# Attention kernel: constant rows on two engines, output weights split once, maxima and sums transposed in one round

## The chip, the cores and the metric

The kernel runs on one core of a Trainium2 chip. The core has five engines with a queue of instructions each: TensorE (PE in the profile; its weight loads are PEld), VectorE (DVE), ScalarE (ACT), GpSimd (POOL) and SyncE (SP), which only issues transfers. Each engine works through its queue in order, and semaphores tie the queues together. The metric is the device time of one execution in microseconds, as the median of several runs.

## The reference

Two kinds of layer alternate, four in all, on an input of 2048 rows of 576 numbers. The change lies in the attention layers.

```python
x = x + _A_ref(_layernorm(x), wqkv, wo)      # attention
x = x + _B_ref(_layernorm(x), w_r, w_i)      # a filter between two Fourier transforms
x = x + _A_ref(_layernorm(x), wqkv, wo)
x = x + _B_ref(_layernorm(x), w_r, w_i)

def _A_ref(x, wqkv, wo):                      # H = 32 heads of Dh = 18, window W = 256
    q, k, v = (x @ wqkv) in 32 heads
    scores = einsum("bhqd,bhkd->bhqk", q, k) * Dh ** -0.5
    scores = where((0 <= i - j) & (i - j < 256), scores, -1e9)
    o = einsum("bhqk,bhkd->bhqd", softmax(scores), v)
    return o @ wo
```

## The kernel before

Every attention layer (`layer_a`) runs three stages, and `layer_b` follows as the fourth.

*The opening* normalizes and transposes the 16 blocks of 128 rows (`xh` and `xl`, the high and low parts of the transposed rows) and computes the values, with one software pipeline over the blocks; `f2` is its last stage.

*The attention loop.* The 32 heads form eight stacks n of four heads (two halves hp of the partitions, two pairs). A stack's queries and keys lie in `qs` and `ks`, at partitions 64 hp and above: 54 rows of split queries or keys, and above them constant rows that memsets have set, 0.0 in `qs` and 1.0 in `ks`. Row 63 of each half of `qs` takes minus the maximum of each query's scores, so that with the row of ones in `ks` one matmul gives the score less its maximum. There are two buffers each of `qs` and `ks`; the memsets are done once per layer, between eight first projections (`proj`, 14 matmul steps each), 64 memsets over the two layers.

The loop runs over time steps t; step t = 16n + i handles block i of stack n. In each step PE does

- four matmuls E (L834) for key block i of stack n against three query blocks i to i+2. ACT takes their exponentials (L835), and POOL cuts off what lies outside the window (L837, L840);
- four matmuls S (L802) for step t+10, whose maxima DVE takes (L804);
- the matmuls U (L854) of exponentials with values for step t-2;
- a few matmul steps `pj` (L741) of later projections, as a table `goal` spreads them. A projection ends in steps 5, 10, 14, 19, 24, 28, 33, 37, 42, 47, 51, 56, 60, 65, 70, 74, 79, 83, 88, 93, 97 and 102. Its result is split on ACT, DVE and POOL, and SP writes it to memory (`qk_d<-sg`, L756).

At every step that is a multiple of 4 SP is also given the twelve `stack_load` transfers (L781) for a chunk of the next stack, `qs<-qk_d` and `ks<-qk_d`; at steps 4 mod 16 the values `vq` as well (L786).

A chunk c is four blocks. Two jobs come once per chunk. `m_rows` transposes the chunk's maxima on PE (`tpm`, L810), ACT negates them into `mt` (L812), and SP writes them into row 63 in four small transfers, `qs<-mt` (L817). They are needed by the E of step 16n + 4c - 2 (16n for the first chunk). `norm` transposes the finished U with its sums (`tpo`, L864), DVE divides (L867, L869), and SP stores the result (`o_d<-o`, L874). Both jobs wait in a list `due`: `m_rows` comes in at steps 2 mod 4, `norm` at steps 3 mod 4. Each step takes at most one job from the list, and none where a projection ends in that step.

*The output stage* (class `Out`) multiplies by the output weights, split into a high and a low part. The split is made in the loop's last steps of each layer: `room` (step 104) loads the raw weights (L474), and at steps 108, 110, 112, 114 and 116 `split` makes one fifth on ACT (L478) and POOL (L479).

The order of all queues is the order of the program text (a manual schedule); nothing is reordered later.

Of the kernel before, what the change touches and what calls it, by code (L numbers as in the profile page):

```python
# [8 lines left out]
F32 = mybir.dt.float32  # L9
F32R = mybir.dt.float32r  # L10
# [5 lines left out]
S, D = 2048, 576  # L16
# [432 lines left out]
class Out:  # L449
# [6 lines left out]
    def room(self):  # L456
        self.rh = rh = self.bp.tile([128, 5 * S], F32R, tag="xh", name="oroom")
        self.rl = f = self.bp.tile([128, 4 * S], F32, tag="xl", name="ofree")
        self.w = {"h": rh[:, 0:2880], "l": rh[:, 2880:5760]}
        self.oT = [rh[:, 5760 + 896 * k:6656 + 896 * k] for k in range(3)]  # L460
        self.oL = [rh[:, 8448 + 256 * k:8704 + 256 * k] for k in range(3)]
        self.gc = rh[:, 9216:9472].rearrange("p (a c) -> p a c", a=2)
        small = f[:, 8130:8170]
        self.st = [small[:, 12 * k:12 * k + 12] for k in range(2)]
        self.mv = [small[:, 24 + 2 * k:26 + 2 * k] for k in range(4)]
        self.rs = [small[:, 32 + k:33 + k] for k in range(4)]
        self.nb = [small[:, 36 + k:37 + k] for k in range(4)]
        self.raw = f[:, 0:2880]
        self.x = [f[:, 576 * k:576 * k + 576] for k in range(5)]
        self.o = [f[:, 2880 + 448 * k:3328 + 448 * k] for k in range(3)]  # L470
        self.tl = [f[:, 4224 + 128 * k:4352 + 128 * k] for k in range(4)]
        self.o7 = f[:, 4736:6784].rearrange("p (n e) -> p n e", n=NT)
        for a, b in ((0, 2), (2, 5)):
            self.nc.sync.dma_start(self.raw[:, a * D:b * D], self.wo_d[:, a * D:b * D])  # L474

    def split(self, k):
        c = slice(k * D, k * D + D)
        self.nc.scalar.copy(self.w["h"][:, c], self.raw[:, c])  # L478
        self.nc.gpsimd.tensor_sub(self.w["l"][:, c], self.raw[:, c], self.w["h"][:, c].bitcast(F32))  # L479

    def consts(self):

# [95 lines left out]
            self.turn(u, tp[:, 0], self.nc.scalar, tp[:, 1, 0:128])  # L578


def layer_a(tc, src, dst, wqk_d, wv_d, wo_d, dc_d, gc_d, dram, copy, wvs, second, spectral):
    nc = tc.nc
    V, A, T, P = nc.vector, nc.scalar, nc.tensor, nc.gpsimd
    SC = float(DH) ** -0.5
# [6 lines left out]
    with ExitStack() as ctx:  # L591
# [30 lines left out]
        with tc.tile_pool(name="a1", bufs=2) as wp, tc.tile_pool(name="a1p", bufs=2, space=PSUM) as pp:  # L622
            if not second:
                wraw = wp.tile([128, 5, D], F32, name="wvraw", bufs=1)
            wh = wp.tile([128, 5, D], F32R, name="wvh", bufs=1)
            wl = wp.tile([128, 5, D], F32R, name="wvl", bufs=1)
            st = wp.tile([128, NT, 2, 6], F32, name="st", bufs=1)
# [50 lines left out]
            def f1(t, h):  # L678
# [5 lines left out]
                if t == 6 and not second:  # L684
                    for j, w in enumerate((wh, wl)):
                        nc.sync.dma_start(wvs[j].bitcast(F32), w.rearrange("p a b -> p (a b)").bitcast(F32))

            def f2(t, h):
                if t in (10, 12):
                    w_split((t - 10) // 2)  # L690
                c = slice(t * 128, (t + 1) * 128)
                ps = pp.tile([128, 2, 512], F32, tag="v", name=f"vps{t}", bufs=2)
                ks = k_steps()
                for i, (wk, p, xk) in enumerate(ks):
                    w = wh if p == "h" else wl
                    for n in range(2):
                        T.matmul(ps[:, n, 0:288], xT(xk, c), w[:, wk, n * 288:(n + 1) * 288],
                                 start=i == 0, stop=i == len(ks) - 1)
                vt = vts[t % 3]
                for n in range(2):  # L700
                    A.copy(vt[:, 16 * n:16 * n + 16, 0:18], ps[:, n, 0:288].rearrange("p (h d) -> p h d", d=18))
                nc.sync.dma_start(v_d[:, :, t].rearrange("n p e -> p n e"), vt.rearrange("p (n h) e -> p n (h e)", n=NQ))
# [4 lines left out]
        with ExitStack() as c2:  # L707
# [8 lines left out]
            qs, ks_ = [], []  # L716
# [159 lines left out]
            for k, (i, c) in enumerate(((0, 0), (1, 0), (0, 1), (1, 1), (0, 2), (0, 3), (1, 2), (1, 3))):  # L876
                for f in proj(i, c, "E" if k % 2 else "pj"):
                    f()

                for b in (32, 96):  # L880
                    P.memset(ks_[i][b:b + 32, :, 512 * c:512 * c + 512].bitcast(F32), 1.0)
                    P.memset(qs[i][b:b + 32, :, 512 * c:512 * c + 512].bitcast(F32), 0.0)
                if k in (2, 4):
                    stack_load(0, k // 2 - 1)
            NX = NQ * NT
# [8 lines left out]
                    goal[t] = 84 + 14 * m - (-14 * (t + 1 - a) // (b - a))  # L894

            OB = NX - 8
            out = Out(nc, ident, eps, bp, ov, o7v, srcv, dstv, wo_d, dc_d, gc_d)

            for t in range(-LEAD, NX + 2):

                if t + LEAD in (0, 2):
                    stack_load(0, 2 + (t + LEAD) // 2)
                n, c = divmod(t + 20, NT)
                if c % 4 == 0 and 0 < n < NQ:
                    stack_load(n, c // 4)
                if t + LEAD == 5:
                    v_load(0)
                if t + 12 in range(NT, NX, NT):
                    v_load((t + 12) // NT)

                want = goal.get(t, len(pj))
                ends = done // 14 != want // 14
                more, done = pj[done:want], want
                for pair in range(2):
                    for hp in range(2):
                        if 0 <= t < NX:
                            exps(t, pair, hp)
                    for hp in range(2):
                        if t + LEAD < NX:
                            score_max(t + LEAD, pair, hp)  # L920
                    while later:
                        later.pop()()
                    if pair == 0 and 0 <= t - 2 < NX:
                        pv(t - 2)
                    if pair == 0 and t < 2:
                        for f in more[:(len(more) + 1) // 2]:
                            f()
                        more = more[(len(more) + 1) // 2:]
                for f in more:
                    f()  # L930
                if copy and t >= 32 and t % 4 == 0 and t < 32 + 16 * len(copy):

                    z, r = divmod(t // 4 - 8, 4)
                    P.dma_start(*[a[32 * r:32 * r + 32] for a in copy[z]])

                y = t + LEAD - 1
                if 0 <= y < NX and y % 4 == 3:
                    due.append((m_rows, *divmod(y // 4, 4)))
                y = t - 3 if t == NX - 2 else t - 4
                if 0 <= y < NX - 1 and y % 4 == 3 and (t != NX - 1):  # L940
                    due.append((norm, *divmod(y // 4, 4)))
                for f, n, c in [] if ends and t >= 2 else due[:1]:
                    f(n, c)
                    due.pop(0)
                if t == OB - 16:
                    out.room()
                if 0 <= t - (OB - 12) < 10 and (t - (OB - 12)) % 2 == 0:
                    out.split((t - (OB - 12)) // 2)
                if t - OB in (0, 1, 2):
                    out.load(t - OB)  # L950
                if t == OB + 3:
                    out.consts()
                    out.last(slice(96, 128), slice(0, 56))
                if t == NX - 1:
                    out.last(slice(0, 96), slice(0, 128))

                if t - OB - 4 in (0, 1, 2, 4):
                    out.tail(min(t - OB - 4, 3))
                if t - OB - 5 in (0, 1, 2):
                    u = t - OB - 5  # L960
                    out.turn(u, pp.tile([128, 512], F32, tag="pj", name=f"tpa{u}", bufs=2), V)
                    if u < 2:
                        out.load(u + 3)
                if t == NX:

                    A.activation(wp.tile([128, 1], F32, name="se", bufs=1), eps, AF.Sqrt)
# [35 lines left out]
def prompt_kernel(tc, x, wqk, wv, wo, w, dc, ic, fc, gc, ga, m2, out):  # L1002
    with tc.tile_pool(name="dram", bufs=1, space=bass.MemoryType.DRAM) as dram, tc.manual_schedule():
        t = [dram.tile([S, D], F32, name=f"x{i}") for i in range(3)]
        cr = {k: dram.tile(list(v.shape), F32R, name=k + "r") for k, v in (("dc", dc), ("ic", ic), ("gc", gc), ("ga", ga))}
        wvs = dram.tile([2, 128, 5 * D], F32R, name="wvs")
        for i, (s, a, d) in enumerate(((x, t[0], t[1]), (t[1], t[2], out))):
            with tc.tile_pool(name=f"dram{i}", bufs=1, space=bass.MemoryType.DRAM) as dr:
                layer_a(tc, s, a, wqk, wv, wo, cr["dc"], cr["gc"], dr, [(cr[k], v) for k, v in (("dc", dc), ("gc", gc), ("ic", ic), ("ga", ga))] if i == 0 else None, wvs, i > 0,
                        lambda *args: layer_b(tc, args[0], d, *args[1:], cr["ic"], fc, cr["ga"], m2, w, dr))  # L1010


# [16 lines left out]
```

## Time and profile before

| | us |
|---|---|
| three timed runs: median (lowest to highest) | 1561.41 (1558.41 to 1566.15) |
| the profiled execution | 1565.98 |
| its span | 1564.3 |
| busy in it: PE, DVE, ACT, POOL | 1427.6, 943.4, 819.4, 753.5 |
| first E of the loop: first layer, second layer | 133.46, 917.98 |

In the profile's lists a group is named by its line, engine and operation, then `out<-in` with the tiles' names; `x` is a count. What stands in brackets is idle time just before, and what ended it. SPq is the queue of SP: the time of such a row is what the issue of a transfer takes on SP, not the transfer itself. The granted clock is that of PE, 1.00 being full speed. Most time steps of the loop take between 2.2 and 4 us.

### The profile page before, as it was taken

What the parts mean: (1) busy time and instruction counts of PE and PEld (TensorE: products, weight loads), DVE (VectorE), ACT (ScalarE), POOL (GpSimd) and SP (SyncE); (2) the same over time, 40 slices, a digit from 0 to 9 for tenths busy, and PEclk for the clock granted to TensorE, in tenths of its full rate; (3) what the DMA queues carried; (4) which work ended last, traced back from release to release, by engine and by line L of the source; (5) the groups of instructions that cost most, each with busy time, mean ns of one, the idle gap of its engine ahead of it and who ended that gap; (6) DMA issues with size and microseconds to landing.
All of it is one profiled execution on the core that took longest, in us unless ns stands there. A gap on an engine that the chain in (4) does not pass through costs nothing. (4 is left out here: it accounts for less than half of the span.)

```text
span 1564.3 us, 35449 instructions
## 1 busy us (share of the span) xinstructions
PE 1427.6 (91%) x12312; PEld 1066.9 (68%) x12312; DVE 943.4 (60%) x3083; ACT 819.4 (52%) x1900; POOL 753.5 (48%) x1240
## 2 busy tenths in 40 slices
PE   7998999999999899877879979999999998998787
PEld 7976666666655799536769756666666567995377
DVE  4337777777774455444543267777787745554445
ACT  5524667666667344224545236666666673442244
POOL 2175556566555333153611755665555563332445
PEclk9999999999988999997979989999999999999889
DMA  6656446555444366666475564545445453656663
GB/s 200 181 180 206 157 154 190 155 168 148 152 130 128 114 199 199 218 198 210 140 235 122 166 208 150 165 147 145 144 131 155 144 145 111 211 194 227 189 209 136
DMA packets 196416, 264.45 MB, mean 169 GB/s; under 512 B 87182, under 2 KB 109326, under 8 KB 195406
## 3 DMA queue, kind: packets, MB, share of 16 engines
q1 hardware_dynamic: 184494, 243.28, 50.2%
q10 hardware_dynamic: 10976, 15.59, 3.0%
q0 software_dynamic: 768, 3.31, 0.8%
q8 instruction: 99, 1.62, 0.4%
q14 instruction: 79, 0.65, 0.1%
HBM read 163.46 MB, written 100.91 MB: 169 GB/s over the span
## 5 line engine op out<-in xcount | busy, mean ns | idle before, releaser
L804 DVE CUSTOM_DVE_ANT_0 jk<-S,mask 128x384 bf16<-128x384 f32 (+2 forms) x1024 | 499.8, 529 | 138.5 <-PE S L802 133.6
L835 ACT ACTIVATE P<-E 128x384 f32<-128x384 f32 (+2 forms) x1024 | 424.6, 475 | 200.0 <-PE E L834 172.1
L837 POOL TENSOR_SCALAR_AFFINE_SELECT P<-P 128x512 f32<-128x512 f32 x256 | 163.1, 637 | 300.6 <-ACT P L835 284.0
L834 PE MATMUL E<-qs,ks 64*128 64x384 f32 (+2 forms) x1024 | 237.9, 416 | 18.3 <-DMA qs<-mt 12.0
L802 PE MATMUL S<-ks,qs 63*128 63x384 f32 (+2 forms) x1024 | 233.2, 367 | 3.0 <-DVE m L804 1.9
L854 PE MATMUL U<-P,vq 128*19 128x128 f32 (+1 forms) x3840 | 205.9, 333 | 1.0 <-POOL P L840 1.0
L834 PEld LDWEIGHTS E<-qs,ks 64*128 64x128 f32 x1024 | 119.7, 186 | 109.5 <-issue 55.6
L741 PE MATMUL pj<-xh,wqh 64*128 64x512 f32 (+1 forms) x640 | 165.3, 405 | 4.3 <-DVE sg L753 2.6
L802 PEld LDWEIGHTS S<-ks,qs 63*128 63x128 f32 x1024 | 130.4, 188 | 41.7 <-DVE m L804 19.2
L854 PEld LDWEIGHTS U<-P,vq 128*19 128x19 f32 x3840 | 90.6, 98 | 97.3 <-issue 36.5
L840 POOL TENSOR_SCALAR_AFFINE_SELECT P<-P 128x512 f32<-128x512 f32 x224 | 142.7, 637 | 0.0
L741 PE MATMUL pj<-xl,wqh 64*128 64x512 f32 (+1 forms) x512 | 127.6, 395 | 0.0
L741 PE MATMUL pj<-xh,wql 64*128 64x512 f32 (+1 forms) x640 | 120.8, 393 | 1.1 <-POOL wql L431 1.1
L527 PE MATMUL ops<-oroom 128*128 128x288 f32 x784 | 113.7, 301 | 4.4 <-DVE oroom L510 3.0
L527 PEld LDWEIGHTS ops<-oroom 128*128 128x128 f32 x784 | 106.6, 191 | 6.2 <-DVE oroom L510 4.0
L171 POOL TENSOR_TENSOR eo<-xn 128x287 f32<-128x287 f32 x32 | 26.2, 818 | 148.4 <-ACT xn L169 148.4
L741 PEld LDWEIGHTS pj<-xh,wqh 64*128 64x128 f32 (+1 forms) x640 | 87.0, 188 | 9.9 <-DVE sg L753 3.3
L804 DVE DVE_READ_ACCUMULATOR2_ANT m<- 128x1 f32 x1024 | 85.2, 83 | 0.0
L199 PE MATMUL pf<-dc,et 128*128 128x290 f32 x384 | 72.3, 313 | 9.7 <-DVE et L190 6.5
L741 PEld LDWEIGHTS pj<-xh,wql 64*128 64x128 f32 (+1 forms) x640 | 71.8, 186 | 9.7 <-POOL wql L431 1.8
L755 POOL TENSOR_TENSOR sg<-sg 128x512 fp32r<-128x512 f32 x56 | 72.1, 1288 | 4.7
L741 PEld LDWEIGHTS pj<-xl,wqh 64*128 64x128 f32 (+1 forms) x512 | 70.5, 189 | 3.8
(179 smaller groups left out, 2567.6 us busy)
## 6 DMA issues: line engine op xcount, KB each, us to landing
qk_d<-sg SPq DMA_DIRECT2D x56, 512.0 KB
qs<-qk_d SPq DMA_DIRECT2D x384, 72.0 KB
ks<-qk_d SPq DMA_DIRECT2D x384, 72.0 KB
v_d<-vt SPq DMA_DIRECT2D x32, 304.0 KB
vq<-v_d SPq DMA_DIRECT2D x16, 608.0 KB
yd<-ye SPq DMA_DIRECT2D x32, 290.0 KB
wt<-in_w SPq DMA_DIRECT2D x16, 580.0 KB
x<-ofree SPq DMA_DIRECT2D x32, 288.0 KB
```

Source lines behind the costliest of these rows:

```text
L171: P.tensor_add(eo[:, 0, 1:288], xn[:, 1:288], xn[:, 575:288:-1])
L199: T.matmul(o, et[:, c, si], m(5 * c + mi), start=q == 0, stop=False)
L527: self.nc.tensor.matmul(self.ps[u][n][:, 0:288], x, self.w[p][:, wk * D + n * 288:wk * D + n * 288 + 288], start=first and i == 0, stop=la ...
L741: T.matmul(ps, w[r, wk], xT(xk, cs)[r], start=s == 0, stop=s == len(ks) - 1)
L755: (P if halves else V).tensor_sub(sg[:, 1], su, sg[:, 0].bitcast(F32))
L802: T.matmul(ps[:, 0:N], q[b:b + 63, pair, i * 128:i * 128 + 128], k[b:b + 63, pair, lo:hi], start=True, stop=True)
L804: V.tensor_tensor_reduce(out=jk[:, 0:N], in0=ps[:, 0:N], in1=mask[:, 384 - N:384], scale=1.0, scalar=-3e38, op0=ALU.add, op1=ALU.max, accu ...
L834: T.matmul(ps[:, 0:nq], k[b:b + 64, pair, j * 128:j * 128 + 128], q[b:b + 64, pair, j * 128:j * 128 + nq], start=True, stop=True)
L835: A.activation(p[:, hl_, 0:nq], ps[:, 0:nq], AF.Exp, scale=SC)
L837: P.affine_select(out=p[:, :, 0:128], in_=p[:, :, 0:128], pattern=[[0, 4], [1, 128]], compare_op=ALU.is_ge, fill=0.0, base=0, channel_mult ...
L840: P.affine_select(out=p[:, :, 256:384], in_=p[:, :, 256:384], pattern=[[0, 4], [-1, 128]], compare_op=ALU.is_gt, fill=0.0, base=0, channel ...
L854: T.matmul(U[32 * h:32 * h + 19, (q0 % 4) * 128:(q0 % 4) * 128 + 128 * (q1 - q0)], vts[n][:, j, h], pt[n, j][:, h, (q0 - j) * 128:(q1 - j) ...
```

## The change

Three edits:

- Of the four memsets that follow each first projection, those at partition 96 are now done by DVE, those at partition 32 by POOL as before.
- The output weights are split in the first layer's opening: a load at block 0, a fifth at blocks 3, 5, 7, 9 and 11, and two writes into a new array `wos` at block 11. In both layers `room` now loads both parts from `wos` into their places, and nothing is split in the loops.
- Between step 2 and the last steps, the list `due` is emptied in one go at steps 3 mod 4 and 0 mod 4 unless a projection ends there, in place of one job per step.

```diff
     def room(self):
-        self.raw = f[:, 0:2880]
-        for a, b in ((0, 2), (2, 5)):
-            self.nc.sync.dma_start(self.raw[:, a * D:b * D], self.wo_d[:, a * D:b * D])
-    def split(self, k):
-        c = slice(k * D, k * D + D)
-        self.nc.scalar.copy(self.w["h"][:, c], self.raw[:, c])
-        self.nc.gpsimd.tensor_sub(self.w["l"][:, c], self.raw[:, c], self.w["h"][:, c].bitcast(F32))
+        for j, w in enumerate("hl"):
+            for a, b in ((0, 2), (2, 5)):
+                self.nc.sync.dma_start(self.w[w][:, a * D:b * D].bitcast(F32), self.wo_d[j, :, a * D:b * D].bitcast(F32))
...
+            def wo_split(k):
+                c = slice(k * D, k * D + D)
+                A.copy(wo[1][:, c], wo[0][:, c].bitcast(F32))
+                P.tensor_sub(wo[2][:, c], wo[0][:, c].bitcast(F32), wo[1][:, c].bitcast(F32))
+                if k == 4:
+                    for j in range(2):
+                        nc.sync.dma_start(wos[j].bitcast(F32), wo[1 + j].bitcast(F32))
             def f2(t, h):
+                if t == 0 and not second:
+                    nc.sync.dma_start(wo[0].bitcast(F32), wo_d)
+                if t in range(3, 13, 2) and not second:
+                    wo_split((t - 3) // 2)
...
                 for b in (32, 96):
-                    P.memset(ks_[i][b:b + 32, :, 512 * c:512 * c + 512].bitcast(F32), 1.0)
-                    P.memset(qs[i][b:b + 32, :, 512 * c:512 * c + 512].bitcast(F32), 0.0)
+                    for a, z in ((ks_, 1.0), (qs, 0.0)):
+                        (V if b == 96 else P).memset(a[i][b:b + 32, :, 512 * c:512 * c + 512].bitcast(F32), z)
...
-                for f, n, c in [] if ends and t >= 2 else due[:1]:
-                    f(n, c)
-                    due.pop(0)
+                if t < 2 or t >= NX - 4 or (t % 4 in (3, 0) and not ends):
+                    for f, n, c in due:
+                        f(n, c)
+                    due.clear()
                 if t == OB - 16:
                     out.room()
-                if 0 <= t - (OB - 12) < 10 and (t - (OB - 12)) % 2 == 0:
-                    out.split((t - (OB - 12)) // 2)
```

SP's queue at steps 16 to 20 of the first layer, before: the chunk of maxima in question is `mt_2`, the third of stack 1; `sg_1` is the result of the projection that ends in step 19, the two rows after it are the stack loads of step 20.

```order
L817 DMA qs_1036<-mt_1_2521 1x4x128 x4
L781 DMA qs_1034<-qk_d 18x2x512 x6
L781 DMA ks_1035<-qk_d 18x2x512 x6
L874 DMA o_d<-o_2_2591 128x4x72
L817 DMA qs_1036<-mt_2_2681 1x4x128 x4
L756 DMA qk_d<-sg_1_2730 128x2x512
L781 DMA qs_1034<-qk_d 18x2x512 x6
L781 DMA ks_1035<-qk_d 18x2x512 x6
L786 DMA vq_2748<-v_d 128x1216
L874 DMA o_d<-o_3_2804 128x4x72
```

The same place now (lines of the changed kernel):

```order
L826 DMA qs_1053<-mt_1_2538 1x4x128 x4
L883 DMA o_d<-o_2_2551 128x4x72
L790 DMA qs_1051<-qk_d 18x2x512 x6
L790 DMA ks_1052<-qk_d 18x2x512 x6
L765 DMA qk_d<-sg_1_2739 128x2x512
L790 DMA qs_1051<-qk_d 18x2x512 x6
L790 DMA ks_1052<-qk_d 18x2x512 x6
L795 DMA vq_2757<-v_d 128x1216
L826 DMA qs_1053<-mt_2_2808 1x4x128 x4
L883 DMA o_d<-o_3_2821 128x4x72
```

`mt_2` has moved from ahead of `sg_1` to behind `sg_1`, the twelve stack loads and `vq`. The same holds for the chunks after the projections that end in steps 47, 51, 79 and 83, with `vq` among them at 51 and 83 alone.

PE's queue at that chunk, before: the maxima are transposed at the end of step 18, and the E that follow are those of step 19.

```order
L741 MATMUL pj_1_0_2511<-xh,wql_1918 128x512
L741 MATMUL pj_1_1_2512<-xh,wql_1918 128x512
L810 MATMUL tpm_2_2679<-ident,m_2_2429 16x128
L834 MATMUL E_0_2688<-qs_1036,ks_1037 128x384
L834 MATMUL E_2_2691<-qs_1036,ks_1037 128x384
```

And now, at the end of step 20; the pair of E that follows is step 21's.

```order
L750 MATMUL pj_2_0_2798<-xh,wqh_1934 128x512
L750 MATMUL pj_2_1_2799<-xh,wqh_1934 128x512
L819 MATMUL tpm_2_2806<-ident,m_2_2446 16x128
L873 MATMUL tpo_3_2814<-ident,us_15_2634 128x128 x4
L843 MATMUL E_0_2825<-qs_1053,ks_1054 128x384
L843 MATMUL E_2_2828<-qs_1053,ks_1054 128x384
```

`tpm_2` has moved by two steps and stands with the sums' `tpo_3`; between it and the E of step 22, which reads this chunk, one step is left where three were.

SP's queue at step 104, before: the store of a result, the raw weights `in_wo`, and the last stack's first `mt`.

```order
L874 DMA o_d<-o_0_7409 128x4x16
L874 DMA o_d<-o_0_7409 128x4x56
L474 DMA ofree<-in_wo 128x1152
L474 DMA ofree<-in_wo 128x1728
L817 DMA qs_1036<-mt_0_7500 1x4x128 x4
```

The same place now:

```order
L474 DMA oroom<-wos 128x1152
L474 DMA oroom<-wos 128x1728
L474 DMA oroom<-wos 128x1152
L474 DMA oroom<-wos 128x1728
L826 DMA qs_1053<-mt_0_7558 1x4x128 x4
```

The two transfers of raw weights ahead of `mt_0` have become four, of both parts, with twice the bytes.

More of the change, by code (lines that the diff above doesn't have):

```diff
@@ L578, in ahead, with layer_a @@
             self.turn(u, tp[:, 0], self.nc.scalar, tp[:, 1, 0:128])
-def layer_a(tc, src, dst, wqk_d, wv_d, wo_d, dc_d, gc_d, dram, copy, wvs, second, spectral):
+def layer_a(tc, src, dst, wqk_d, wv_d, wo_d, dc_d, gc_d, dram, copy, wvs, wos, second, spectral):
     nc = tc.nc
@@ L624, in layer_a @@
                 wraw = wp.tile([128, 5, D], F32, name="wvraw", bufs=1)
+                wo = [wp.tile([128, 5 * D], F32R, name=f"wo{k}", bufs=1) for k in range(3)]
             wh = wp.tile([128, 5, D], F32R, name="wvh", bufs=1)
@@ L896, in layer_a @@
             OB = NX - 8
-            out = Out(nc, ident, eps, bp, ov, o7v, srcv, dstv, wo_d, dc_d, gc_d)
+            out = Out(nc, ident, eps, bp, ov, o7v, srcv, dstv, wos, dc_d, gc_d)
             for t in range(-LEAD, NX + 2):
@@ L1005, in prompt_kernel @@
         cr = {k: dram.tile(list(v.shape), F32R, name=k + "r") for k, v in (("dc", dc), ("ic", ic), ("gc", gc), ("ga", ga))}
-        wvs = dram.tile([2, 128, 5 * D], F32R, name="wvs")
+        wvs, wos = [dram.tile([2, 128, 5 * D], F32R, name=k) for k in ("wvs", "wos")]
         for i, (s, a, d) in enumerate(((x, t[0], t[1]), (t[1], t[2], out))):
             with tc.tile_pool(name=f"dram{i}", bufs=1, space=bass.MemoryType.DRAM) as dr:
-                layer_a(tc, s, a, wqk, wv, wo, cr["dc"], cr["gc"], dr, [(cr[k], v) for k, v in (("dc", dc), ("gc", gc), ("ic", ic), ("ga", ga))] if i == 0 else None, wvs, i > 0,
+                layer_a(tc, s, a, wqk, wv, wo, cr["dc"], cr["gc"], dr, [(cr[k], v) for k, v in (("dc", dc), ("gc", gc), ("ic", ic), ("ga", ga))] if i == 0 else None, wvs, wos, i > 0,
                         lambda *args: layer_b(tc, args[0], d, *args[1:], cr["ic"], fc, cr["ga"], m2, w, dr))
```

## Prediction

> **What bounds the kernel now.** I read the windows first (busy time of each engine in stretches of the span), then the transfer queue's timeline, then matmul by matmul around the places that the change touches.
>
> ```profile
> span 1564.3 us, 35449 instructions
> 240.00:280.00 40.00, 40.00 (x437) 25.27 (x436) 31.03 (x120) 27.41 (x67) 24.47 (x37) 1.00 0.58 175
> 86.00:120.00 34.00, 32.99 (x192) 26.74 (x190) 14.74 (x49) 7.72 (x14) 33.06 (x37) 1.00 0.61 204
> ```
>
> The columns after the length are the busy microseconds of PE, weight loads, DVE, ACT and POOL, then the granted clock, the DMA share and GB/s. In the attention loop (240 to 280) PE is busy all 40.00 us at full clock; DVE has 9 us free, ACT 13, POOL 16. So the loop is bound by PE, and whatever makes PE wait there is paid in full. In the eight first projections (86 to 120) PE is busy 32.99 of 34.00 us, POOL 33.06, DVE 14.74.
>
> **A row of maxima that comes too late costs PE its whole wait, and the trace has two such waits.**
>
> ```profile
> 139.75 0.39 SPq L756 DMA_DIRECT2D qk_d<-sg  x1
> 140.23 2.54 SPq L817 DMA_DIRECT2D qs<-mt  x4
> 142.99 1.00 PE L834 MATMUL E<-qs,ks 64*128 64x384 f32 x2 [4.79 <-DMA qs<-mt]
> 926.11 2.47 SPq L817 DMA_DIRECT2D qs<-mt  x4
> 929.67 1.02 PE L834 MATMUL E<-qs,ks 64*128 64x384 f32 x2 [6.91 <-DMA qs<-mt]
> ```
>
> At time step 2 of each layer the four small transfers of `mt` stood behind others in SP's queue; PE's next E matmul started 2.76 us (142.99 - 140.23) and 3.56 us (929.67 - 926.11) after the first of the four was issued, and PE had stood still for 4.79 and 6.91 us. SP issues in program order, so what stands ahead of `mt` there decides.
>
> **The change, part by part. 1: the joined rounds.** Before, the maxima of a chunk are transposed at time steps 2 mod 4; now at 3 mod 4, together with the sums, and at 0 mod 4 where a projection ends in that step. The E matmuls that read the chunk come at step 16n+4c-2, 2 mod 4 again. At step 3 mod 4 two whole steps are left, and nothing new stands ahead on SP: I price that at nothing (cover: two steps of PE work; without it, a wait as in the third part). But projections end at steps 19, 47, 51, 79 and 83, all 3 mod 4. There the round moves by two steps to 20, 48, 52, 80, 84, which leaves one step, and as the order rows shown with the change say, the four `mt` transfers move on SP behind the projection's write-back, twelve stack loads and, at three of the five, `vq`. In the trace of before SP does this around step 20:
>
> ```profile
> 193.93 2.46 SPq L817 DMA_DIRECT2D qs<-mt  x4
> 199.54 0.39 SPq L756 DMA_DIRECT2D qk_d<-sg  x1
> 200.03 2.48 SPq L781 DMA_DIRECT2D qs<-qk_d  x6
> 202.56 3.65 SPq L781 DMA_DIRECT2D ks<-qk_d  x6
> 206.91 0.38 SPq L874 DMA_DIRECT2D o_d<-o  x1
> 202.13 0.47 PE L834 MATMUL E<-qs,ks 64*128 64x384 f32 x2
> ```
>
> The last row is the E of step 22, the first that needs this chunk. Before, the `mt` transfers went out at 193.93. Now they go out where `o_d` does, at 206.91 at the earliest: 4.78 us after PE is there. What paces SP between 199.54 and 206.91 (the split of the projection on POOL, the transfers in flight) does not depend on the moved work. At the other four places of the first layer, and at one of the second:
>
> ```profile
> 283.08 0.45 PE L834 MATMUL E<-qs,ks 64*128 64x384 f32 x2
> 287.06 0.38 SPq L874 DMA_DIRECT2D o_d<-o  x1
> 294.58 0.47 PE L834 MATMUL E<-qs,ks 64*128 64x384 f32 x2
> 299.42 0.38 SPq L874 DMA_DIRECT2D o_d<-o  x1
> 375.61 0.45 PE L834 MATMUL E<-qs,ks 64*128 64x384 f32 x2
> 379.69 0.39 SPq L874 DMA_DIRECT2D o_d<-o  x1
> 387.12 0.45 PE L834 MATMUL E<-qs,ks 64*128 64x384 f32 x2
> 392.06 0.38 SPq L874 DMA_DIRECT2D o_d<-o  x1
> 1162.17 0.44 PE L834 MATMUL E<-qs,ks 64*128 64x384 f32 x2
> 1165.34 0.39 SPq L874 DMA_DIRECT2D o_d<-o  x1
> ```
>
> SP is free 3.98, 4.84, 4.08 and 4.94 us after PE; with 4.78 the five make 22.6 us. The second layer's row has 3.17 where the first has 4.08, so I take 20 us for its five (ends 15.9 and 22.6). To each of the ten comes the time from first issue to E, 2.76 to 3.56 us above, I take 3.2: 32 us. **Waits: 22.6 + 20 + 32 = 75 us.** Ends: an issue of 0.6 us and an instant landing give 43 + 6 = 49; a wait for all four transfers (2.5 us more each) gives about 100. Behind the waiting E stands all of PE, and behind that ACT's exponentials and DVE's maxima. Nothing of the lost time is made up, since PE is the bound.
>
> **2: the clock after each wait.**
>
> ```profile
> 929.60:933.00 3.40, 3.33 (x14) 2.89 (x16) 1.98 (x7) 1.75 (x4) 0.76 (x2) 0.50 0.71 221
> 933.00:936.40 3.40, 3.40 (x28) 1.38 (x27) 1.15 (x6) 1.14 (x3) 0.47 (x1) 0.58 0.58 165
> ```
>
> After the 6.91 us wait PE ran at a granted clock of 0.50 and then 0.58, about 6.2 us at half clock in these 6.8 us. If PE were limited by its clock alone there, that costs 3.1 us; if by others, nothing. Ten waits: 0 to 31 us; I take the middle, **15 us**. The Trainium skill's page "TensorE: Matmul & The Clock Gate", Part 1, says that the clock falls to half after an idle window of about 3.4 us and returns after a busy one as long; the granted clock of 0.50 agrees, and by that rule alone (3.4 to 6.8 us at half clock after each wait) the term would be 17 to 34 us.
>
> **3: what a joined round saves on PE.**
>
> ```profile
> 239.17 0.56 PE L741 MATMUL pj<-xh,wqh 64*128 64x512 f32 x2
> 239.41 0.56 PE L741 MATMUL pj<-xl,wqh 64*128 64x512 f32 x2
> 239.90 0.28 PE L810 MATMUL tpm<-ident,m 128*16 128x128 f32 x1
> 240.11 0.44 PE L834 MATMUL E<-qs,ks 64*128 64x384 f32 x2
> 242.69 0.66 PE L864 MATMUL tpo<-ident,us 128*128 128x128 f32 x4
> 243.27 0.44 PE L834 MATMUL E<-qs,ks 64*128 64x384 f32 x2
> ```
>
> A round of one transposition takes 0.21 us from its start to the next E, one of four takes 0.58: three more cost 0.37, 0.12 each. So the last transposition's change back to E costs 0.21 - 0.12 = 0.09 us that a joined round pays once, and I take the same for the change into it: about 0.17. Of 32 rounds of maxima per layer 29 are joined, 58 in all: **-10 us**. Ends: nothing, and the whole lone round (240.11 - 239.41 - 0.24 = 0.46 us, 0.24 being the step from one pj row to the next) 58 times, 27 us.
>
> **4: the output weights.** Ten casts on ACT and ten subtractions on POOL leave the ends of the two loops; five of each come into the first opening, with one 1.47 MB load and two writes.
>
> ```profile
> 435.70:480.20 44.50, 42.44 (x342) 22.64 (x340) 30.71 (x121) 27.12 (x69) 23.38 (x32) 0.77 0.34 95
> 1222.20:1259.20 37.00, 35.00 (x342) 19.27 (x339) 30.46 (x119) 26.70 (x68) 23.36 (x32) 1.00 0.39 113
> 454.17 0.67 ACT L478 CAST oroom<-ofree 128x576 fp32r<-128x576 f32 x1 [1.16 <-DMA ofree<-in_wo]
> L478 ACT CAST oroom<-ofree 128x576 fp32r<-128x576 f32 x10 | 6.7, 667 | 1.2 <-DMA ofree<-in_wo 1.2
> L479 POOL TENSOR_TENSOR oroom<-ofree,oroom 128x576 fp32r<-128x576 f32 x10 | 14.1, 1410 | 0.9 <-ACT oroom L478 0.8
> ```
>
> The first two rows are the same 14 time steps (103 to 116) in the two layers, with the same 342 matmuls: 44.5 us at a clock of 0.77 in the first, 37.0 us at 1.00 in the second. In the first, ACT stood 1.16 us for the raw weights, with the exponentials queued behind it, just before the clock fell. With no cast in the loop this wait is gone, and I expect the clock to hold: **-7.5 us** (ends 0 and -7.5). Of the ACT casts themselves (6.7 us) DVE, busy 30.46 of 37.00 us, hides most: **-2** (ends 0 and -6.7). In the opening, ten instructions of these prices are 5 x (0.67 + 1.41) = 10.4 us on two engines beside PE's matmuls, which cover them; if ACT or DMA falls behind, some shows: **+1.5** (ends 0 and 10.4). The two loads per layer become four, 2.95 MB, ahead of the last stack's first `mt` on SP, and its last `mt` comes one short step later: **+2** together (ends 0 and one 6.91 us wait per layer).
>
> **5: the memsets.**
>
> ```profile
> L881 POOL MEMSET ks<- 32x1024 f32 x32 | 30.3, 948 | 1.4
> L722 DVE MEMSET U<- 128x512 f32 x2 | 1.0, 485 | 13.9 <-ACT vt L701 13.9
> SPq L781 <- DMA qk_d<-sg: 51.8, 28, 8.9
> ```
>
> Half of 64 memsets leave POOL, 15.2 us per layer, which is the whole of its fullness from 86 to 120. But SP's first stack load waited up to 8.9 us for the projection's write-back, not for POOL, so nothing on the path starts sooner: **0** (ends 0 and the 4.79 and 6.91 us waits at step 2, should they vanish). On DVE 512 elements took 485 ns, so a memset there is about 0.97 us and 16 of them 15.5 us per layer, into 19.3 us that DVE has free.
>
> **The sum.** 75 + 15 - 10 - 7.5 - 2 + 1.5 + 2 + 0 = +74 us. The profiled execution took 1565.98 us (its span and 1.7 us around it); that gives 1640, and since it lay 4.6 us above the median of the three timed runs (1561.41), I forecast **1635 us**.
>
> **The rivals.**
> - *The moved rows arrive in time.* If the ten waits come to less than 17 us together, under 1.7 us each, the change pays: without them the sum is -10 - 7.5 - 2 + 1.5 + 2 = -16, **1545 us**, faster. For it: 22 of 32 chunks per layer move without harm, and the other engines have time. Against it: SP reaches the moved transfers 3 to 5 us after PE needs them at every row quoted. Chance 0.07.
> - *The waits are there but short:* the first transfer lands at once and the clock does not fall. 49 - 16 = +33, **1594 us**. Against it: in both waits of the trace E started 2.76 and 3.56 us after the issue. Chance 0.13.
> - *The waits are longer and the clock takes its full price:* rows queue behind `vq` in the rings, 85 to 100 us of waits and 31 of clock, less 16: +100 to +115, **1661 to 1676 us**. The quoted waits had no `vq` ahead of them; the three places per layer with one may be worse. Chance 0.14.
> - *The forecast itself,* 1605 to 1660: 0.66.
>
> **How the numbers follow.** The chances stand with the cases above. The range reaches from the short waits to the long ones, **1590 to 1675**, and leaves out the first rival and the outer ends. Faster by over 0.5% (8 us, about what a measurement of this kernel can tell from no change) 0.06, within it 0.02, slower 0.92.
>
> **What would show it.** PE should wait in E for `qs<-mt` at ten new places, at steps 22, 50, 54, 82 and 86 of each layer, 5 to 9 us each; the releaser's total, 12.0 us before, should be near 85. The granted clock should fall to 0.50 after each. SP should issue `mt` there after `ks<-qk_d` or `vq`. The first layer's steps 103 to 116 should take 37 us at a clock of 1.00, with no `in_wo` wait on ACT. The wait at step 2 should stay within 2 us of 4.79 and 6.91. I am wrong if `mt` goes out before the stack loads at those five steps, if E does not wait for it, or if PE makes up the lost time.

## The result and the profile after

The changed kernel takes **1649.74 us** (median of 4 runs, 1647.48 to 1653.98) against 1560.97 us before (4 runs): ratio **1.057**, 95% interval 1.053 to 1.060. The forecast was 1635 us, range 1590 to 1675.

The changed kernel's page gives the span and PE's costliest group, E, with the idle time ahead of it; below them, two of its waits of PE (total us, times, longest):

```profile
span 1648.1 us, 35452 instructions
L843 PE MATMUL E<-qs,ks 64*128 64x384 f32 (+2 forms) x1024 | 243.3, 412 | 93.6 <-DMA qs<-mt 87.7
```

```profile
PE E L843 <- DMA qs<-mt: 87.7, 20, 9.7
PE S L811 <- DVE m L813: 6.6, 4, 3.1
```

The row of the kernel before:

```profile
PE E L834 <- DMA qs<-mt: 12.0, 3, 6.9
```

PE now waits 87.7 us for rows of maxima, 12.0 before. The timeline around step 22 of the first layer (start us, us, engine, line, names, and in brackets the wait and what ended it), first SP's queue, then PE:

```profile
201.66 0.38 SPq L765 DMA_DIRECT2D qk_d<-sg  x1
202.14 2.44 SPq L790 DMA_DIRECT2D qs<-qk_d  x6
204.63 3.54 SPq L790 DMA_DIRECT2D ks<-qk_d  x6
208.27 0.35 SPq L795 DMA_DIRECT2D vq<-v_d  x1
208.72 2.46 SPq L826 DMA_DIRECT2D qs<-mt  x4
211.27 0.39 SPq L883 DMA_DIRECT2D o_d<-o  x1
```

```profile
201.19 0.28 PE L819 MATMUL tpm<-ident,m 128*16 128x128 f32 x1
203.17 0.44 PE L843 MATMUL E<-qs,ks 64*128 64x384 f32 x2
212.82 1.05 PE L843 MATMUL E<-qs,ks 64*128 64x384 f32 x2 [8.33 <-DMA qs<-mt]
```

The maxima were transposed at 201.19 us. Their rows left SP only at 208.72, when write-back, twelve stack loads and `vq` had been issued, and PE stood still for 8.33 us. The same wait is at steps 22, 50, 54, 82 and 86 of both layers: 8.33, 6.35, 9.50, 6.26, 8.79 us and 9.30, 6.00, 9.18, 5.79, 9.65 us, **79.2 us** together. At 50 and 82, where no `vq` stands ahead, it is some 3 us shorter. At all ten places the granted clock falls to 0.50, for 6.8 to 13.7 us.

The windows of the same kernel: the half clock around that wait, the four us after, a quiet stretch of the loop, the first projections, and steps 103 to 116 of each layer (length, then busy us of PE, weight loads, DVE, ACT and POOL, then clock, DMA share, GB/s):

```profile
206.60:216.80 10.20, 3.98 (x28) 2.78 (x30) 1.00 (x8) 1.47 (x4) 0.00 (x0) 0.50 0.43 134
216.80:220.80 4.00, 4.00 (x46) 2.52 (x42) 2.00 (x12) 2.95 (x8) 3.64 (x5) 0.99 0.00 0
330.00:370.00 40.00, 39.80 (x438) 25.55 (x438) 32.83 (x124) 27.66 (x69) 25.00 (x38) 1.00 0.42 130
86.00:120.00 34.00, 31.04 (x157) 26.55 (x155) 24.62 (x46) 6.98 (x12) 16.93 (x21) 0.90 0.61 196
483.21:520.20 36.99, 34.27 (x342) 18.78 (x339) 30.77 (x121) 24.66 (x65) 17.76 (x28) 1.00 0.51 162
1304.94:1341.99 37.05, 34.07 (x343) 18.74 (x340) 30.70 (x119) 24.72 (x65) 17.76 (x28) 1.00 0.52 161
```

The spell of half clock lasts 10.2 us, but PE works in only 3.98 of them: the clock falls while PE still waits, and the wait hides the rest. Between the places PE is as full as before (39.80 of 40.00 us). Steps 103 to 116 take 37.0 us in both layers. In the first projections POOL is down to 16.93 us and DVE up to 24.62, and PE is busy 1.95 us less (32.99 before), with a new wait of 2.96 us in that window, shown further down.

Where the span's 83.9 us came from, by the start of E at each step, after less before:

| stretch | layer 1 | layer 2 |
|---|---|---|
| start of the layer to step 12 (layer 2: from step 127 of layer 1) | +3.3 | -0.5 |
| 20 to 24, 48 to 56, 80 to 88: the ten waits | +48.8 | +49.7 |
| 12 to 20, 24 to 48, 56 to 80, 88 to 103 | -4.6 | -6.3 |
| 103 to 117 | -7.5 | 0.0 |
| 117 to 127, and behind layer 2 | -0.2 | +1.2 |

### The profile page after: what moved, and what is told of

It reads as the page before. It is cut to its first block, busy times and chain, and to the rows that moved or that the text cites. A ratio compares the mean times of both kernels' runs of the same rounds, so it can differ in the third digit from the quotient of the medians.

```text
span 1648.1 us, 35452 instructions
## 1 busy us (share of the span) xinstructions
PE 1431.6 (87%) x12312; PEld 1086.0 (66%) x12312; DVE 973.0 (59%) x3115; ACT 817.0 (50%) x1895; POOL 714.8 (43%) x1203
## 5 line engine op out<-in xcount | busy, mean ns | idle before, releaser
L843 PE MATMUL E<-qs,ks 64*128 64x384 f32 (+2 forms) x1024 | 243.3, 412 | 93.6 <-DMA qs<-mt 87.7
L843 PEld LDWEIGHTS E<-qs,ks 64*128 64x128 f32 x1024 | 128.0, 191 | 186.4 <-issue 121.9
L811 PE MATMUL S<-ks,qs 63*128 63x384 f32 (+2 forms) x1024 | 238.6, 374 | 7.6 <-DVE m L813 6.6
L863 PE MATMUL U<-P,vq 128*19 128x128 f32 (+1 forms) x3840 | 209.5, 338 | 0.1
L750 PE MATMUL pj<-xh,wqh 64*128 64x512 f32 (+1 forms) x640 | 171.0, 417 | 4.3 <-DVE sg L762 2.6
L750 PE MATMUL pj<-xl,wqh 64*128 64x512 f32 (+1 forms) x512 | 133.7, 408 | 0.0
L750 PE MATMUL pj<-xh,wql 64*128 64x512 f32 (+1 forms) x640 | 127.7, 411 | 0.0
L750 PEld LDWEIGHTS pj<-xh,wqh 64*128 64x128 f32 (+1 forms) x640 | 91.2, 195 | 9.6 <-DVE sg L762 3.3
L750 PEld LDWEIGHTS pj<-xh,wql 64*128 64x128 f32 (+1 forms) x640 | 78.7, 200 | 7.6
L750 PEld LDWEIGHTS pj<-xl,wqh 64*128 64x128 f32 (+1 forms) x512 | 75.4, 197 | 3.7
```

What stands on the lines that cost most here:

```text
L750: T.matmul(ps, w[r, wk], xT(xk, cs)[r], start=s == 0, stop=s == len(ks) - 1)
L811: T.matmul(ps[:, 0:N], q[b:b + 63, pair, i * 128:i * 128 + 128], k[b:b + 63, pair, lo:hi], start=True, stop=True)
L843: T.matmul(ps[:, 0:nq], k[b:b + 64, pair, j * 128:j * 128 + 128], q[b:b + 64, pair, j * 128:j * 128 + nq], start=True, stop=True)
L863: T.matmul(U[32 * h:32 * h + 19, (q0 % 4) * 128:(q0 % 4) * 128 + 128 * (q1 - q0)], vts[n][:, j, h], pt[n, j][:, h, (q0 - j) * 128:(q1 - j) ...
```

## The experiments

The theory: the late rounds alone cost the time, since SP issues their rows behind the stack loads. The rivals: the weights or memsets share in it; one step between a round and its E is too short whatever SP does. Each ratio below is against the kernel before, timed on the same chip (medians 1563 to 1565 us).

**The old rule for the rounds, weights and memsets kept**

```diff
-                if t < 2 or t >= NX - 4 or (t % 4 in (3, 0) and not ends):
-                    for f, n, c in due:
-                        f(n, c)
-                    due.clear()
+                for f, n, c in [] if ends and t >= 2 else due[:1]:
+                    f(n, c)
+                    due.pop(0)
```

> The changed kernel with the rule of before for the due rounds; the memsets on two engines and the output weights kept in DRAM stay. Theory (the moved rounds alone cost the time): the ten waits of E for the rows of maxima go, PE waits for them only at step 2 of each layer, and the weights and memsets are worth -7.5 us (steps 103 to 116 of the first layer at 37 us) and 0 to +5 us (opening and lead): 1553 to 1561 us. Rival (the two loads per layer that became four, or the memsets ahead in DVE's queue, push the rows back too): waits of E stay outside step 2, and the time is above 1580 us.

Measured: 1559.41 us, ratio 0.997 (0.995 to 0.999). None of the ten waits is left, and the time is in the theory's range. **The new rule alone**, the same edit the other way round in the kernel before:

> The kernel before with only the new rule for the due rounds. Theory: the ten waits are all there, 70 to 85 us, with the clock at half after each; less what the joined rounds save and with the new wait at step 10: 1640 to 1660 us, as long as the whole change or a few us longer, since the first layer's steps 103 to 116 keep their 44.5 us. Rival (weights and memsets make a good part of the loss): under 1625 us.

Measured: 1662.65 us, ratio 1.062 (1.058 to 1.066), 2.7 us above the range of the theory. Its wait of PE for the rows:

```profile
PE E L834 <- DMA qs<-mt: 90.8, 17, 9.9
```

So the rule carries the whole loss. The weights and memsets together are worth 0.3% on the good side. The wait at step 10 was expected here and is not in this trace, while the old rule with weights and memsets has it (1.66 us); of that below.

**Lone rounds at the five places, joined ones elsewhere**

```diff
-                if t < 2 or t >= NX - 4 or (t % 4 in (3, 0) and not ends):
+                early = t % 4 == 2 and not ends and want // 14 != goal.get(t + 1, len(pj)) // 14
+                if t < 2 or t >= NX - 4 or early or (t % 4 in (3, 0) and not ends):
```

> The changed kernel, but where a projection ends in the next step the maxima are transposed alone at 2 mod 4, as before; the other rounds stay joined at 3 mod 4. Theory (only the five places per layer where a projection ends at 3 mod 4 cost): the ten waits go and the joined rounds keep their gain, 48 rounds at 0.2 to 0.45 us each (-10 to -20 us), with -7.5 us in the first layer's steps 103 to 116, and +3 to +9 us from the opening, the lead and the new wait at step 10: 1533 to 1555 us, faster than both kernels. Rival (a joined round at 3 mod 4 is itself too late for the E two steps on, whatever SP does): E waits at most chunks, and the time is over 1575 us.

Measured: **1552.81 us, ratio 0.992** (0.989 to 0.995), faster than both kernels. Its SP queue at the same place, and PE's E of step 22:

```profile
197.48 2.44 SPq L826 DMA_DIRECT2D qs<-mt  x4
202.36 0.39 SPq L765 DMA_DIRECT2D qk_d<-sg  x1
202.85 2.43 SPq L790 DMA_DIRECT2D qs<-qk_d  x6
```

```profile
202.47 0.45 PE L843 MATMUL E<-qs,ks 64*128 64x384 f32 x2
```

The rows go out 5 us ahead of E, and nothing waits there. In the four quiet stretches of the table, where 28 pairs of lone rounds became joined ones, this kernel is 9.4 us faster than before: 0.33 us each.

**The next stack's loads and `vq` behind the rounds of the same step**

```diff
-                n, c = divmod(t + 20, NT)
-                if c % 4 == 0 and 0 < n < NQ:
-                    stack_load(n, c // 4)
...
-                if t + 12 in range(NT, NX, NT):
-                    v_load((t + 12) // NT)
...
                     due.clear()
+                n, c = divmod(t + 20, NT)
+                if c % 4 == 0 and 0 < n < NQ:
+                    stack_load(n, c // 4)
+                if t + 12 in range(NT, NX, NT):
+                    v_load((t + 12) // NT)
```

> The changed kernel with the loads of the next stack and of vq behind the due rounds of the same step, so that at steps 20, 48, 52, 80 and 84 the rows of maxima are issued on SP behind the write-back of the projection but ahead of the twelve stack loads. Theory (it is the order on SP, stack loads and vq above all): in the trace of before the write-back goes out at 199.54 us and E of step 22 starts at 202.13; rows issued right behind it would make E wait 1 to 2 us there, ten such waits 10 to 20 us, too short for the clock to fall: 1545 to 1570 us. Rival (one step between the round and its E is too short in itself, or the write-back is what holds SP): waits of 4 us and more at the ten places, with half clock, over 1600 us.

Measured: 1567.73 us, ratio 1.002 (0.999 to 1.005). The rounds still run at step 20, one step ahead of their E:

```profile
203.00 0.38 SPq L765 DMA_DIRECT2D qk_d<-sg  x1
203.48 2.46 SPq L826 DMA_DIRECT2D qs<-mt  x4
206.03 0.39 SPq L883 DMA_DIRECT2D o_d<-o  x1
206.53 2.18 SPq L790 DMA_DIRECT2D qs<-qk_d  x6
```

```profile
206.11 0.41 PE L843 MATMUL E<-qs,ks 64*128 64x384 f32 x1 [0.29 <-DMA qs<-mt]
```

Behind the write-back but ahead of the loads, the rows let E start 2.6 us after their issue, and no wait at the ten places reaches 1 us. That the join is one step late costs little; the stack loads and `vq` ahead of it cost the 79 us. But the time is 1.002 of before, where the lone rounds reach 0.992, and the reason is open. Rounds at steps 26, 42 and 74 of the first layer wait 1.2 to 1.8 us, yet those at 42 and 74 wait in kernels with the old order of the loads too (1.52 us at 42 in the changed kernel, 2.10 and 1.36 us in one further down), and the profiled execution, 1580.42 us, was one of this kernel's longest.

**A joined round at every 3 mod 4**, also where a projection ends (`t % 4 == 3` in place of the two last conditions): ahead of the next step's loads, behind the write-back.

> The changed kernel with the joined round at every step 3 mod 4, also where a projection ends there: at those five places per layer the rows stand on SP behind the projection's write-back but ahead of the next step's stack loads and vq. Theory (the stack loads cost, not the write-back): waits of E at the ten places under 2 us as with the loads put behind (there 0.4 to 1.2 us), no half clock, 1548 to 1568 us. Rival (the write-back, which waits for POOL's split, is what holds SP): waits of 3 us and more there, over 1590 us.

Measured: 1561.84 us, ratio 1.000 (0.997 to 1.003). No wait there is over 1.2 us, as expected; the two tests agree.

**The late rounds' rows from ACT's queue**

```diff
-                        nc.sync.dma_start(q[b:b + 1, pair, c * 512:c * 512 + 512].rearrange("a (t q) -> a t q", t=4).bitcast(F32),
+                        (nc.scalar if t > 8 and t % 4 == 0 else nc.sync).dma_start(q[b:b + 1, pair, c * 512:c * 512 + 512].rearrange("a (t q) -> a t q", t=4).bitcast(F32),
```

> The changed kernel with nothing moved in time, but the four transfers of a round that runs at 0 mod 4 (the five late places per layer) are issued from ACT's queue instead of SP's. Theory (what stands ahead on SP makes the ten waits): in the changed kernel SP issued the rows of step 20 at 208.72 us, behind 6.1 us of stack loads and the vq load; from ACT they go out right after its copy, and E waits 0 to 2 us; ACT pays some 2.5 us of issuing per place (SP needs 2.46 us for four) and has 13 of 40 us free: 1545 to 1575 us. Rival (one step between the round and its E is too short whatever the queue): waits of 4 us and more at the ten places with half clock after them, over 1600 us.

Measured: 1592.91 us, ratio 1.019 (1.015 to 1.024), above the range of the theory and below the rival's. Its ACT queue at step 20, and PE's next E:

```profile
201.27 0.27 ACT L821 ACTIVATE mt<-tpm 16x128 fp32r<-16x128 f32 x1 [0.62 <-PE tpm L819]
201.57 3.09 ACTq L826 DMA_DIRECT2D qs<-mt  x4
204.76 0.87 ACT L844 ACTIVATE P<-E 128x384 f32<-128x384 f32 x2 [3.23 <-DMA qs<-mt]
```

```profile
205.31 0.44 PE L843 MATMUL E<-qs,ks 64*128 64x384 f32 x1 [1.95 <-ACT P L844]
```

The waits for the rows at the ten places are gone, so it was SP's order. But ACT issues for 3.09 us with the exponentials queued behind it, and PE waits 1.95 us for them one step earlier, 1.3 to 1.5 us at five more places: a new wait in place of the old. The stretches of the ten waits still grew by 24.5 us; PE's waits in them come to 12.7, and six spells of 3.4 us at a granted clock of 0.50 lie there, worth 10 us at most by an estimate from their length. And E now waits 1.5 to 3.2 us for the next rows that go by SP, at steps 58 and 90. The Trainium skill's page "DMA: Bandwidth & Descriptors", section "Issuing engines are not separate DMA queues", says that issuing from several engines saves only the time of issuing; here that time, 3.09 us on an engine with its own work, was the price.

**The memsets alone, and the weights alone**, each put into the kernel before:

> The kernel before with only the memsets on two engines. Theory (the memsets on VectorE, not the output weights, make what is new in the lead): the first S waits some 3 us for DVE's maxima in each layer with the clock at half after it, the wait at step 10 (1.7 us in the first layer with the old rule and all the rest) is there, and in exchange the waits of 4.79 and 6.91 us at step 2 shrink below 2 us; the first layer is 2 to 5 us later at step 12, the second 2 to 5 us less; steps 103 to 116 of the first layer stay at 44 us: 1557 to 1567 us. Rival (the weights' transfers make the step 10 wait and the late start): no wait at step 10 and no late start.

> The kernel before with only the output weights split once and kept in DRAM. Theory: steps 103 to 116 of the first layer at 37 us (-7.5), the opening +0.5 to +3 us, the waits at step 2 stay at 4 to 7 us and none is new at step 10: 1550 to 1560 us. Rival (the clock at the end of the first layer falls for another reason than the wait for the raw weights): those steps stay at 44 us and the time is 1560 to 1566 us.

Memsets: 1564.56 us, ratio 1.001 (0.999 to 1.004). Weights: 1559.79 us, ratio 0.997 (0.995 to 1.000), which this measurement can barely tell from no change. With the memsets on two engines the fourth S of the loop waits 2.99 us in the first layer for DVE to finish with the first (the expectations call it the first S), E of step 0 comes 5.0 and 4.1 us later, and the waits at step 2 shrink from 4.79 and 6.91 to 1.99 and 3.26 us: by step 12 the first layer is 1.2 us behind, the second unchanged, less either way than the 2 to 5 us expected. **The wait at step 10 is in neither trace**, so the expectation was wrong there. It stands in most kernels that have the weights together with the new rule or the memsets (1.4 to 2.5 us in the first layer). What tips it was not settled.

With the weights alone, steps 103 to 116 of the first layer took 42.10 us, not 37. Its row of PE at step 112, and the window behind:

```profile
461.27 0.83 PE L843 MATMUL E<-qs,ks 64*128 64x384 f32 x2 [1.05 <-DMA qs<-mt]
```

```profile
462.30:476.00 13.70, 13.70 (x83) 7.64 (x84) 8.38 (x33) 7.28 (x17) 4.31 (x8) 0.50 0.07 13
```

A wait of 1.05 us, and then 13.70 us at half clock. Over all traces of this study these steps took 41.0 to 46.5 us in five of the six layers with the splits in the loop (mean 43.0), and 36.5 to 39.6 us in eighteen of the twenty-two without (40.9 to 43.6 in the others, mean 38.3). The long ones have a short wait in common. In the layers with the splits, ACT waited for the raw weights in five of the six, 0.72 to 2.04 us, and these are the five long ones; the sixth, the second layer of the kernel before (37.07 us), has no such wait. In the four long layers without the splits E waited 0.90 to 1.43 us for rows of maxima at step 106 or 112; in the other eighteen no wait of E at these steps was over 0.97 us. This is a pattern over 28 layers; no run changed such a wait alone.

**The lone rounds at five places with all memsets on POOL; the same, and the rows of the lead from ACT's queue; and that one with memsets on two engines**

> The kernel of the lone rounds at five places (joined elsewhere) with all memsets on POOL again. Theory (memsets on VectorE gain nothing over both layers): the waits at step 2 come back at 4 to 7 us, the waits of S for DVE and of E at step 10 go, and the time is within 4 us of that kernel's 1552.8 us, 1546 to 1556 us. Rival (the memsets are the better half of what is left): 1557 us or more.

> The kernel with lone rounds at five places, joined rounds elsewhere, the weights kept in DRAM and all memsets on POOL; in addition the rows of maxima of the rounds before step 8 go out from ACT's queue. Theory (the waits at steps 2 and 10 are SP's queue too, which issues without a pause from 146 to 164 us): they vanish, 2.5 + 1.4 us in the first layer and 5.4 in the second with some clock behind them, 5 to 13 us less than the 1555.6 us of that kernel without this edit: 1543 to 1551 us. Rival (the rows are late there because the transfers already in the rings hold them: at step 10 E started 6.6 us after the first was issued): the waits stay, 1552 us or more.

> As the kernel before in this call, but with the memsets on two engines. Theory (the memsets delay the first maxima on DVE by some 3 us per layer, and gain only by a shorter wait at step 2, which now is gone anyway): 2 to 8 us slower than that kernel. Rival (POOL's fullness in the lead holds the split of the projections and so the loads): as fast or faster.

The first: 1555.59 us, ratio 0.995 (0.992 to 0.997), where the theory put it, though a wait of 1.36 us at step 10 stayed in its first layer. The second and third: 1578.35 us (1.009, 1.006 to 1.012) and 1585.42 us (1.014, 1.009 to 1.018), slower by what was meant to be a gain, the second far above the 1543 to 1551 us expected; that the third is 7 us above the second is as expected. In the second the waits at steps 2 and 10 are gone, but now E waits for ACT:

```profile
PE E L843 <- ACT P L844: 16.6, 24, 2.0
PE E L843 <- DMA qs<-mt: 3.1, 6, 1.2
```

Steps 2 to 8 are 8.1 us longer than before in each layer. Its timeline shows ACT idle for 7.25 us ahead of the first exponentials, where the kernel without this edit has 3.77:

```profile
140.28 1.64 ACT L844 ACTIVATE P<-E 128x384 f32<-128x384 f32 x4 [7.25 <-DMA qk_d<-sg]
```

Of the 7.25 us, ACT spends 2.53 issuing four transfers of rows; the end of the idle time the profile puts down to a projection's write-back, and why ACT waits for that was not settled. The profiled execution took 1570.41 us, so this trace shows only part of the loss in the median.

**Memsets on two engines for the first four projections only**, with the lone rounds at five places:

```diff
-                        (V if b == 96 else P).memset(a[i][b:b + 32, :, 512 * c:512 * c + 512].bitcast(F32), z)
+                        (V if b == 96 and k < 4 else P).memset(a[i][b:b + 32, :, 512 * c:512 * c + 512].bitcast(F32), z)
```

> The kernel of the lone rounds at five places with the memsets on two engines for the first four projections only; those after the last four are all on POOL. Theory (the memsets on VectorE hurt by standing just ahead of the first maxima in DVE's queue, not by their work): the first S waits less than 1 us for DVE's maxima in both layers (3 us before), no half clock at 111 us, the first E comes 2 to 5 us sooner, of which the wait at step 2 takes back some: 1546 to 1554 us, a ratio to before of 0.988 to 0.994. Rival (what counts is the wait for the rows at step 2, which takes back all that comes sooner): the ratio is that of the kernels with two engines or with POOL alone, 0.992 to 0.997.

Measured: 1553.66 us, ratio 0.994 (0.991 to 0.996). The fourth S waits 0.32 us instead of 3.75:

```profile
108.60 0.33 PE L811 MATMUL S<-ks,qs 63*128 63x128 f32 x1 [0.32 <-DVE m L813]
```

Against the lone-round kernel with memsets on two engines throughout, E of step 0 comes 7.0 us sooner in the first layer and 1.7 us in the second, but the waits at step 2 are back at 4.85 and 4.69 us. So the theory holds for the place and the rival for a good part of the value: at step 12 the first layer has 4.1 us left, the second is some 1 us later, and the ratio lies inside the intervals of the two kernels beside it. Which of the three placements of the memsets is best stays open.

## Why the prediction was right, step by step

- **The waits: right in place and total, with one term too small.** Forecast 75 us at ten named steps, measured 79.2. How long after PE the first of the four transfers goes out was forecast at 42.6 us for the ten and came to 40.0 (3.2 to 5.2 each). From there to E 3.2 us were taken, from two waits with no `vq` ahead: it was 2.4 to 2.7 us at the four places without `vq` and 4.1 to 5.5 at the six with it, 39.2 us in place of 32. This is what the third rival named, short of its 85 us; that `vq` holds the rows is read from these places and was not tested by itself. The total came closer than its terms, since the first was too large by 2.6 us. Moving only the loads, or only the rounds, removes the waits.
- **The clock behind them: right.** Forecast 15 us; the ten stretches grew by 98.5 us, 19 more than the waits (23 with what their ten joined rounds save, at 0.33 us each). In the window shown, the spell is longer than supposed (10.2 us against 6.2), but only 4 us of it are work. Over the ten, 3.8 to 7.2 us of each spell lie behind the start of E, 51 us in all, which at half the clock costs 26 us at most, by an estimate from these lengths. The 19 to 23 us are most of that, where the forecast took half, and the clock falls during the wait and not after it.
- **The joined rounds: the mechanism right, the size too small.** 0.17 us each was put together from the starts of single rows on PE, as the cost of changing into and out of the transpositions; counted over whole stretches it is 0.33 us, which would be 19 us for 58 rounds in place of 10. It lies inside the forecast's ends (nothing to 0.46 us each).
- **The weights: right in this pair of traces, and more general than told.** The first layer's steps came out 7.48 us shorter, and ACT's wait for the raw weights stood in every long layer with the splits. But the size is one draw: both layers run at half clock there in some executions, and without the splits rarely. The mean of the traces, 43.0 less 38.3, is 4.7 us per layer. The -2 us for ACT's casts did not come: steps 103 to 116 of the second layer, at full clock before and after, took the same time (37.07 and 37.05). Of the +2 us for the four loads and the last rows, waits of 0.29 and 0.22 us at step 112 are seen; in the kernel with the weights alone that wait is 1.05 us, ahead of the half clock.
- **The opening: right or smaller.** Five casts and five subtractions lie beside PE's work; the first projection's start moved from 81.37 to 81.85 us.
- **The memsets: the price right, the cover wrong.** DVE had 19.3 us free and got 14.6 per layer, but in its queue order:

```profile
109.46 0.91 DVE L891 MEMSET ks<- 32x1024 f32 x1 [0.27 <-issue]
110.54 0.91 DVE L891 MEMSET qs<- 32x1024 f32 x1 [0.16 <-issue]
111.48 0.29 DVE L813 CUSTOM_DVE_ANT_0 jk<-S,mask 128x128 bf16<-128x128 f32 x1
```

```profile
111.83 0.47 PE L811 MATMUL S<-ks,qs 63*128 63x128 f32 x1 [2.96 <-DVE m L813]
```

  The last two memsets stand just ahead of the first maxima, and PE waits 2.96 us. The waits at step 2, which were to stay within 2 us of 4.79 and 6.91, shrank to 1.31 and 0.77: that sign was wrong. The lead's delay had moved, and the net of 0 came about by a later start and a shorter wait at step 2, neither of them forecast; with the memsets alone it is 1.2 and 0.2 us at step 12.
- **The wait at step 10** (2.49 and 1.09 us) was not in the forecast, which priced a move to 3 mod 4 at nothing.

The total came out 15 us above the forecast. The profiled executions differ by 83.9 us where the sum said 74: 4.2 more for the waits, 4.3 for the clock (net of joined rounds), 2 for ACT's gain that did not come, 0.3 for the lead and the rest, and 0.9 less in the quiet stretches. The other 5 us are the step from the profiled execution to the median: it was 4.6 us for the kernel before, and 0.1 us (1649.87 against 1649.74) for the changed one.

## What to carry to other kernels

Joining two small jobs on one engine can move the transfer that follows one of them behind others in another queue: list what each transfer newly stands behind, from its ready time to the first reader, before counting what the join saves. Joining only where nothing new stands ahead kept the saving here (ratio 0.992). Free time of an engine covers new work only if that work does not stand ahead of something awaited in its queue. And a transfer moved to the queue of a busy engine takes that engine's time: 3.09 us of issuing on ACT were followed by a wait of PE of 1.95 us.

## What the runs showed that was not expected

- A wait of PE as short as 1.05 us was followed by 13.7 us at a clock of 0.50, while the wait of 8.33 us was followed by 4 us of work at half clock. The Trainium skill's page "TensorE: Matmul & The Clock Gate", Part 1, ties the fall to an idle window of about 3.4 us; the long wait agrees, the short one does not. Nor is it alone: a wait of 2.10 us at step 42 of another kernel was followed by 3.4 us at 0.50, and in the first layer of the kernel before the clock fell in steps 103 to 116 with no wait of PE over 0.64 us in them. Why these steps fall so easily was not tested.
- At step 10 the rows reach E long after their issue. With the old rule, weights and memsets, the timeline has

```profile
161.21 2.58 SPq L826 DMA_DIRECT2D qs<-mt  x4
168.88 1.05 PE L843 MATMUL E<-qs,ks 64*128 64x384 f32 x2 [1.66 <-DMA qs<-mt]
```

  7.7 us from issue to E, against 2.6 us (loads behind the rounds) and 4.1 us (changed kernel) at step 22 of the first layer. So SP is not what holds the rows there; what does, behind the issue, was not tested.
